# Which engine's queue issues the stores of gV and gK: GpSimd or ScalarE

## The chip, the cores and the metric

The kernel runs on one core of a Trainium2 chip. The core has five engines that run side by side, each with its own queue of instructions: TensorE (PE; its weight loads are PEld), VectorE (DVE), ScalarE (ACT), GpSimd (POOL) and SyncE (SP). An instruction that waits holds up everything behind it in its engine's queue. A transfer between the chip's large memory and the on-chip tiles is issued by an instruction of SP, ACT or POOL and then carried out by 16 DMA engines that all issuers share. The metric is the device time of one execution in microseconds (us).

## The reference

The reference computes one decode step of a transformer block and all its gradients. A query (batch 2, one position, width 640) goes through a layer norm and a projection into 32 heads of 128, attends to caches of 4096 keys and values per head, is projected back and added to x, and goes through a layer norm and a small relu network. What is computed around the change are the gradients of the caches. For one pair (b, h):

```python
scores = einsum("bhqd,bhkd->bhqk", q, k) * (Dh ** -0.5)
p = softmax(scores)
o = einsum("bhqk,bhkd->bhqd", p, v)
```

With one query position, the gradient of v is the outer product of p (4096) and the gradient of o (128), and the gradient of k is the outer product of the scores' gradient (4096) and q (128). Each is a matrix of 4096 x 128 bf16, 1 MiB. There are 64 pairs, so 128 such matrices are written: 134 MB of the 149 MB that the kernel writes. It reads 211 MB, most of it the caches, V being read a second time for 52 of the pairs.

## The kernel before

A tile of 1 MiB is [128 partitions, 32 chunks, 128], 8 KB in each partition.

**Pass 1** (p1_iter, L461) walks over the 64 pairs with three of them in work at a time: pair i has its K transposed on PE and copied out of PSUM by ACT (t_sb, L440) and its scores computed; pair i-1 has its softmax (ep on ACT, L523) and K times ep on VectorE (pk, L476); pair i-2 has its matrix with V on PE (m_ps, L469). It yields between eight segments, k = 0 to 7.

**Pass 2** (p2_iter, L858, and p2_tail, L837) makes the gradients, in the order of the list turns. p2_iter(j) transposes V of its pair (tile W) in four groups on PE, each copied out by ACT (T0 to T3, L440), and multiplies each with the gradient of o (dp). Meanwhile VectorE writes gV in two halves (L832, by outer_half). The dp of the pair is complete only after T3; p2_tail(j) then makes gsp on VectorE (L843) and gK in two halves (L832). p2_tail(j) is run from inside p2_iter(j+1). In the first steps without pass 1, ACT writes the last eight of the 32 chunks of gV (nsb, L899), in the last three steps four.

POOL issues the store of gV at L900 and that of gK at L851, straight behind the last instruction that writes the tile in the program's order, and copies the small tiles pp and pf for the next step (L874, L877). The buffers of gV and gK come from a pool of tiles with the tag "g": take hands one out and give returns it to the list in program order; on the chip, the next writer of the buffer waits until its store has landed. There are three of them while both passes run, and five to ten later.

The order of the work is written out by hand. The plan (L1110) is a list of steps (i, j): pass 1 alone until i = 40, then both, with a new j at every second i; in the last two steps of pass 1 (i = 64 and 65) j = 12 and 13; then pass 2 alone (i is None) from j = 14 on. While both run, p2_step (L1163) is called after chosen segments of p1_iter (HEAVY, LIGHT). In the background, generators do the weights' gradients: outer_rows (L939) has PE make blocks of 512 columns, ACT copy them into ot (L965), and ACT issue their stores (L968, 19 of them). go_group, ga_gen and gx_gen keep VectorE busy with products and sums (L658).

SP issues all loads (L456 for K, V and W). When a buffer comes free, the next load is issued.

Of the kernel before, what the change touches and what calls it, by code (L numbers as in the profile page):

```python
# [15 lines left out]
def kernel(  # L16
# [73 lines left out]
    def take(tag, shape, name):  # L90
        assert free[tag] > 0, (tag, name)
        free[tag] -= 1
        k = homes[tag].pop(0)
        t = pools[k].tile(shape, BF16, tag=f"big{k}", bufs=1, name=name)
        home_of[id(t)] = (tag, k, t)
        return t
# [354 lines left out]
    def natural(cache, b, h):  # L451
        return cache[b, h].rearrange("(p sc) d -> p sc d", sc=NSC)
# [8 lines left out]
    def p1_iter(i, dve_group, busy):  # L461
# [56 lines left out]
            m_part(0)  # L518
            m_part(1)
        yield  # L520
        if p is not None:
            ep = pkp.tile([128, NSC, 2], BF16, tag="ep", bufs=3, name="ep")
            nc.scalar.activation(out=ep[:], in_=p["s"][:, :, None].to_broadcast([128, NSC, 2]),  # L523
                                 func=ACT.Exp, bias=nb[:], scale=SCALE, accum_out=es[:, bp, hp:hp + 1])
            p["ep"] = ep
            p["pk"] = []
            pk_tile(0)
        if c is not None:
            c["KT2"] = pair_transpose(c["K"], 2, busy=busy)
# [304 lines left out]
            in0=row.rearrange("p (a two) -> p a two", two=2)[:, None, :, :].to_broadcast([128, n, 64, 2]),  # L834
            in1=colp[:, sl, None, :].to_broadcast([128, n, 64, 2]), op=ALU.mult)

    def p2_tail(j):  # L837

        p = S2[j]
        bp, hp = turns[j]  # L840
        pair_matvec(p["dp"], p.pop("T3"), 3, gom[:, bp, hp, :, :])
        gsp = small.tile([128, NSC, 2], BF16, tag="gsp", bufs=2, name="gsp")
        nc.vector.scalar_tensor_tensor(  # L843
            out=gsp[:], in0=p["dp"][:, :, None].to_broadcast([128, NSC, 2]), scalar=negdot[:, hp, bp:bp + 1],
            in1=P_bf[:, p_slot[(bp, hp)], :, None].to_broadcast([128, NSC, 2]), op0=ALU.add, op1=ALU.mult)
        yield
        gK = take("g", [128, NSC, 128], "gK")
        outer_half(gK, p["rb"][:, 128:256], gsp, 0)
        yield
        outer_half(gK, p["rb"][:, 128:256], gsp, 1)  # L850
        nc.gpsimd.dma_start(out=natural(out_2, bp, hp), in_=gK[:])  # L851
        give(gK)
        del S2[j]
        yield

    NSB = 8

    def p2_iter(j, nsb):  # L858

        tail = p2_tail(j - 1) if j - 1 in S2 and "T3" in S2[j - 1] else iter(())  # L860
        c = S2[j]
        next(tail, None)
        b, h = turns[j]
        go = gom[:, b, h, :, :]
        bank = pst([128, 512], FP32, "sps", "dp_ps")
        for k, col in enumerate((goc, qsc)):
            nc.tensor.matmul(bank[:, 128 + k * 128:256 + k * 128],  # L867
                             lhsT=col[:, h, b:b + 1].to_broadcast([128, 128]), rhs=ident_bf[:],
                             start=True, stop=True)
        c["dp"] = bank[:, 0:NSC]  # L870
        rb = mats.tile([128, 256], BF16, tag="rb", bufs=3, name="rb")
        nc.scalar.activation(out=rb[:], in_=bank[:, 128:384], func=ACT.Copy, scale=rt[:, b, h:h + 1])  # L872
        pp = small.tile([128, NSC, 2], BF16, tag="pp", bufs=2, name="pp")
        nc.gpsimd.tensor_copy(out=pp[:], in_=P_bf[:, p_slot[(b, h)], :, None].to_broadcast([128, NSC, 2]))  # L874
        if nsb:
            pf = small.tile([128, NSB], FP32, tag="pf", bufs=2, name="pf")
            nc.gpsimd.tensor_copy(out=pf[:, 0:nsb], in_=P_bf[:, p_slot[(b, h)], NSC - nsb:NSC])  # L877
        c.update(rb=rb, pp=pp)
        c["T0"] = pair_transpose(c["W"], 0)
        next(tail, None)  # L880
        yield
        for _ in tail:
            yield
        c["T1"] = pair_transpose(c["W"], 1)
        pair_matvec(c["dp"], c.pop("T0"), 0, go)
        yield
        c["T2"] = pair_transpose(c["W"], 2)
        pair_matvec(c["dp"], c.pop("T1"), 1, go)
        yield
        c["T3"] = pair_transpose(c["W"], 3)  # L890
        give(c["W"], "g" if j < H and j != 1 and owned["g"] < 3 else None)
        pair_matvec(c["dp"], c.pop("T2"), 2, go)
        gV = take("g", [128, NSC, 128], "gV")
        outer_half(gV, c["rb"][:, 0:128], c["pp"], 0)
        yield
        outer_half(gV, c["rb"][:, 0:128], c["pp"], 1, HALF - nsb)
        if nsb:
            for k in range(nsb):
                nc.scalar.activation(out=gV[:, NSC - nsb + k, :], in_=rb[:, 0:128], func=ACT.Copy, scale=pf[:, k:k + 1])  # L899
        nc.gpsimd.dma_start(out=natural(out_3, b, h), in_=gV[:])  # L900
        give(gV)
        yield


# [265 lines left out]
    for n, (i, j) in enumerate(plan):  # L1170
        all_go = all(("go", B - 1, h) in done for h in range(H))
        if i is None and plan[n - 1][0] is not None:
            pkp.release()
            big1 = tc.alloc_tile_pool(name="big1", bufs=1)
            for _ in range(2):
                more_home("ld", big1)
            share(ld=KEPT[1] + 4, g=5)
        if all_go and not late[0]:
            wop.release()
            big3 = tc.alloc_tile_pool(name="big3", bufs=1, side="right")  # L1180
            for tag in ("ld", "g", "g", "q", "q", "q"):
                more_home(tag, big3)
        late[0] = all_go
        more = int(late[0])
        if fin is not None and not bg2 and not bg3:
            share(ld=8 + 3 * more, g=7 + 3 * more)
        elif fin is not None and j >= H:
            held = sum(bh in kept for bh in turns[j + 1:])
            share(ld=5 + held + more, g=5 + 2 * more, f=3, q=2 + 3 * more)
        while g2 is not None:  # L1190
            p2_step()
        open_tail = [k for k in S2 if "T3" in S2[k]]
        if j is not None:
            if j < NP1:
                bg_until(("go", *turns[j]))
            nsb = 0 if i is not None else NSB if j < H and fin is None else NSB // 2 if j >= NP1 - 3 else 0
            g2 = p2_iter(j, nsb) if j < NP1 else p2_tail(NP1 - 1)
        elif open_tail:
            g2 = p2_tail(open_tail[0])
        if i is None and ("w1", 1) in done and fin is None:  # L1200
            wts.release()
            fin = tc.alloc_tile_pool(name="fin", bufs=1)
            big2 = tc.alloc_tile_pool(name="big2", bufs=1)
            more_home("f", big2)
            banks.update(sps=[2, 3], o=[4, 5, 6])
            bg2.append(("fin", fin_gen(fin)))
            bg3.append(("gx", gx_gen(fin)))
        if i == 12:
            bg.append(("ga", ga_gen()))
        if i == H + 2:  # L1210
            banks["bc"].insert(0, banks["sps"].pop(0))
        elif i == P2_AT:
            banks["bc"].remove(7)
            banks["sps"].insert(0, banks["bc"][0])
            banks["bc"] = [7]
        rate = RATES[0 if i is not None and i <= H + 1 else 1 if j is None and i < P2_AT else
                     2 if i is not None else 3 if j <= H else 4]
        if i is None:
            spread[0] = 2
            at_k[0] = 1  # L1220
            k = 0
            while g2 is not None:
                p2_step()
                pump()
                slot[0] = int(k in ((1, 3, 5) if j <= H else (1, 4)))
                k += 1
                bg_step(0, rate)
                bg_step(1, RATE2[int(j >= RATE2_AT)] * (0.4 if spreading[0] else 1.0))
                bg_step(2, RATE3)
            continue  # L1230
        at = LIGHT if j is None else HEAVY_TAIL if open_tail else HEAVY
        for k, _ in enumerate(p1_iter(i, i < H + 1, 0)):
            for _ in range(at.get(k, 0)):
                if g2 is not None:
                    p2_step()
            if k == 5:
                a_heads(i)
            pump()

            spread[0] = 1 if i < P2_AT else 2  # L1240
            at_k[0] = k
            if i >= P2_AT:
                slot[0] = int(k == 6 or (k == 1 and j is None))
            elif i > H + 1:
                slot[0] = {1: 2, 3: 1, 4: 1, 6: 1}.get(k, 0)
            else:
                slot[0] = int(k in (1, 6))
            bg_step(0, rate)
            bg_step(1, 0.0)
        if i is not None and i in (H + 1, NP1 + 1):  # L1250
            bg.append((f"m{i // H - 1}", middle_gen(i // H - 1)))
# [41 lines left out]
```

## Time and profile before

| what | value |
|---|---|
| median of 3 runs | 894.84 us (894.83 to 897.51) |
| the profiled execution | 896.3 us |
| its span on the core | 894.4 us |
| busy: PE, DVE, ACT, POOL | 740.6, 688.1, 469.5, 198.6 us |
| bytes read, written | 211.1 MB, 149.1 MB |
| mean rate over the span | 405 GB/s |
| POOL's DMA queue | 134.2 MB |
| SP's DMA queue | 211.1 MB |
| ACT's DMA queue | 14.9 MB |

The profile is one execution recorded by the hardware. Its page gives each engine's busy time, then the span in 40 equal slices: each digit is the busy share of a slice in tenths, and the lines DMA and GB/s give the mean busy share of the 16 DMA engines and what they moved. Then come the DMA queues, the chain of work that ended last, the costliest groups of instructions (a line L440 is line 440 of the kernel, and t_sb<-t_ps says what is written from what), and the DMA issues with the median time from issue to landing. The same trace can be asked for a line, for a stretch of time, or for all instructions of a stretch in order; there, "[0.56 <-PE t_ps L435]" means that the engine sat idle for 0.56 us until an instruction of PE at L435 was done.

### The profile page before, as it was taken

To read this page: it belongs to the slowest core of one execution; us is meant where nothing else is said; L and a number is where in the kernel's file an instruction comes from. 1 tells how busy PE (TensorE), PEld (TensorE's weight loads), DVE (VectorE), ACT (ScalarE), POOL (GpSimd) and SP (SyncE) were. 2 spreads that over 40 slices of the span, in tenths; PEclk is the share of its full clock that TensorE was granted. 3 is DMA by queue.
4 is the path that set the end of the run, shared out by engine and by line. 5 is a ranking of instruction groups with operands and counts; after the bars stand their busy time and mean duration, and the time that the engine had idled before them with its cause. 6 is when DMAs were issued, how large, how long until landed. Compare 5 with 4: busy or idle time off the path is not lost.

```text
span 894.4 us, 24636 instructions
## 1 busy us (share of the span) xinstructions
PE 740.6 (83%) x10145; PEld 622.7 (70%) x10145; DVE 688.1 (77%) x1283; ACT 469.5 (52%) x1184; POOL 198.6 (22%) x342
## 2 busy tenths in 40 slices
PE   4999899999998998897867887875698988858881
PEld 4887788888887887777757776764566765635570
DVE  2666778976888897796678897877988468898992
ACT  1344334443555665464545776553476666537751
POOL 1344434442210000000011231111222111111141
PEclk9999989999999999898995555555657566555655
DMA  9999999999979999999999999999999999999996
GB/s 377 420 412 403 409 407 418 411 414 410 356 299 366 422 422 424 422 422 423 414 382 390 416 416 418 414 412 422 398 394 423 426 421 424 423 426 424 423 423 256
DMA packets 56304, 361.84 MB, mean 405 GB/s; under 512 B 5696, under 2 KB 11904, under 8 KB 15488
## 3 DMA queue, kind: packets, MB, share of 16 engines
q1 hardware_dynamic: 34536, 211.13, 58.1%
q0 software_dynamic: 18432, 134.23, 36.1%
q10 hardware_dynamic: 3224, 14.92, 4.0%
q8 instruction: 80, 1.31, 0.6%
q14 instruction: 32, 0.26, 0.1%
HBM read 211.11 MB, written 149.13 MB: 403 GB/s over the span
## 4 chain that ended last, share of the span: by engine, by line
DMA 37%; PE 31%; DVE 19%; issue 6%; ACT 3%; POOL 1%; SPq 0%; POOLq 0%; DVEq 0%; ACTq 0%
DMA out_dram<-gK 16%; PE t_ps L435 13%; DMA Vt<-in_A_v_cache_dram 12%; PE m_ps L469 7%; DMA out_dram<-gV 5%; DVE gV L832 5%; DVE gK L832 4%; DVE rows L658 4%; PE s_ps L448 3%; DVE pk L476 3%; DMA wo_t<-in_A_wo_dram 2%; PE u_ps L498 2%; DMA Kt<-in_A_k_cache_dram 2%; PE dp_ps L448 2%; ACT t_sb L440 1%
## 5 line engine op out<-in xcount | busy, mean ns | idle before, releaser
L440 ACT COPY t_sb<-t_ps 128x512 f32<-128x512 f32 x479 | 272.6, 587 | 181.3 <-PE t_ps L435 177.0
L448 PEld LDWEIGHTS <-t_sb 128*128 128x128 bf16 x4096 | 169.7, 103 | 75.1 <-ACT t_sb L440 33.3
L435 PE MATMUL t_ps<-ident_f,Wt 128*128 128x128 f32 x832 | 200.0, 392 | 0.4 <-ACT t_sb L440 0.4
L476 DVE TENSOR_TENSOR pk<-Kt,ep 128x2048 bf16<-128x2048 bf16 x128 | 156.3, 1222 | 44.7 <-ACT ep L523 26.0
L469 PE MATMUL m_ps<-pk,Vt 128*128 128x129 bf16 x2048 | 175.8, 224 | 15.0 <-DMA Vt<-in_A_v_cache_dram 14.4
L832 DVE TENSOR_TENSOR gK<-rb,gsp 128x2048 bf16<-128x2048 bf16 x128 | 153.4, 1224 | 18.5 <-DMA out_dram<-gV 16.9
L832 DVE TENSOR_TENSOR gV<-rb,pp 128x2048 bf16<-128x2048 bf16 (+2 forms) x128 | 147.1, 1172 | 23.6 <-DMA out_dram<-gK 23.1
L435 PEld LDWEIGHTS t_ps<-ident_f,Wt 128*128 128x128 f32 x832 | 140.2, 204 | 32.1 <-issue 26.5
L435 PE MATMUL t_ps<-ident_f,Kt 128*128 128x128 f32 x1024 | 153.4, 285 | 3.7 <-DMA Kt<-in_A_k_cache_dram 3.5
L469 PEld LDWEIGHTS <-Vt 128*128 128x128 bf16 x2048 | 130.9, 100 | 18.1 <-DMA Vt<-in_A_v_cache_dram 16.1
L435 PEld LDWEIGHTS t_ps<-ident_f,Kt 128*128 128x128 f32 x1024 | 116.3, 148 | 5.1 <-issue 2.6
L486 POOL COPY pk<-ep 128x16 bf16<-128x16 bf16 x80 | 83.6, 1047 | 152.3 <-ACT ep L523 107.0
L448 PE MATMUL dp_ps<-gom,t_sb 128*128 128x2 bf16 x2048 | 96.0, 168 | 14.5 <-ACT t_sb L440 14.1
L900 POOL DMA_DIRECT2D out_dram<-gV x64 | 34.3, 536 | 317.7 <-DVE gV L832 115.6
L448 PE MATMUL s_ps<-gom,t_sb 128*128 128x2 bf16 x2048 | 80.2, 164 | 1.2 <-DVE t_sb L438 1.2
L851 POOL DMA_DIRECT2D out_dram<-gK x64 | 34.1, 533 | 200.3 <-DVE gK L832 149.6
L582 ACT CAST MT<-m_ps 128x128 bf16<-128x128 f32 x64 | 17.0, 266 | 116.3 <-PE m_ps L469 116.3
L965 ACT CAST ot<-o_ps 128x512 bf16<-128x512 f32 (+3 forms) x152 | 66.8, 494 | 8.9 <-DMA out_dram<-ot 7.3
L872 ACT ACTIVATE rb<-dp_ps,rt 128x256 bf16<-128x256 f32 x64 | 30.3, 474 | 45.5 <-PE dp_ps L867 43.2
L658 DVE CUSTOM_DVE_ANT_0 rows<-wo_t,rows 128x640 bf16<-128x640 bf16 x64 | 52.3, 818 | 0.2
L658 DVE CUSTOM_DVE_ANT_0 rows<-wqs,gqr 128x1024 bf16<-128x1024 bf16 x40 | 48.8, 1220 | 0.2
L658 DVE CUSTOM_DVE_ANT_0 rows<-w_t,rows 128x640 bf16<-128x640 bf16 (+2 forms) x58 | 45.9, 792 | 2.8 <-ACT rows L636 2.1
(194 smaller groups left out, 715.7 us busy)
## 6 DMA issues: line engine op xcount, KB each, us to landing
Kt<-in_A_k_cache_dram SPq DMA_DIRECT2D x64, 1024.0 KB, 16.5
Vt<-in_A_v_cache_dram SPq DMA_DIRECT2D x64, 1024.0 KB, 16.6
out_dram<-gV POOLq DMA_DIRECT2D x64, 1024.0 KB, 14.1
out_dram<-gK POOLq DMA_DIRECT2D x64, 1024.0 KB, 14.3
Wt<-in_A_v_cache_dram SPq DMA_DIRECT2D x52, 1024.0 KB, 11.4
out_dram<-ot ACTq DMA_DIRECT2D x6, 960.0 KB, 12.7
wq_t<-in_A_wq_dram SPq DMA_DIRECT2D x5, 1024.0 KB, 11.0
wqs<-in_A_wq_dram SPq DMA_DIRECT2D x5, 1024.0 KB, 22.2
```

The source lines that it names most:

```text
L435: nc.tensor.transpose(t_ps[:, j, :], natf[:, 2 * cc:2 * cc + 2, :].rearrange("p c k -> p (c k)"), ident_f[:])
L440: nc.scalar.copy(out=t_sb[:], in_=t_ps[:])
L448: nc.tensor.matmul(dst[:, sc:sc + 2], lhsT=v[:, j, :, par], rhs=vecs[:, par, :], start=(par == 0), stop=(par == 1))
L469: nc.tensor.matmul(r["m"][:, 0:129], lhsT=r["V"][:, sc, :], rhs=r["pk"][sc // HALF][:, sc % HALF, 0:129], start=(sc == 0), stop=(sc == NSC ...
L476: nc.vector.tensor_tensor(out=p["pk"][k][:, :, 0:128].rearrange("p s (a two) -> p s a two", two=2), in0=p["K"][:, sl, :].rearrange("p s (a ...
L486: nc.gpsimd.tensor_copy(out=col, in_=e)
L658: nc.vector.tensor_tensor_reduce(out=junk[0:kc, 0:width], in0=in0, in1=in1, scale=1.0, scalar=0.0, op0=ALU.mult, op1=ALU.add, accum_out=acc)
L832: nc.vector.tensor_tensor(out=pairs_view(dst[:, sl, :]), in0=row.rearrange("p (a two) -> p a two", two=2)[:, None, :, :].to_broadcast([128 ...
L851: nc.gpsimd.dma_start(out=natural(out_2, bp, hp), in_=gK[:])
L872: nc.scalar.activation(out=rb[:], in_=bank[:, 128:384], func=ACT.Copy, scale=rt[:, b, h:h + 1])
L900: nc.gpsimd.dma_start(out=natural(out_3, b, h), in_=gV[:])
L965: nc.scalar.copy(out=ot[0:P, k, n0:n0 + nn], in_=o_ps[0:P, 0:nn])
```

## The change

No store of gV or gK is issued where its tile is finished any more. The tile and its destination are put on a list, unsent, and a function send issues everything on that list from ACT's queue and gives the tiles back. send is called in four places:

- in p1_iter, in the third segment (k = 2), behind ep's activation, or in the same place where there is no pair i-1;
- in p2_iter when pass 1 is over (lone): once behind the copy of T0, which finds the gV of the step before, and once behind the copy of T2, which finds the gK of the step before;
- in the last p2_tail, behind gsp for the last gV;
- in the last p2_tail, behind the second half of gK for the last gK.

What is computed, and the number and shape of the stores, stay the same; POOL keeps its copies.

```diff
+            send()
             pk_tile(0)
...
+    unsent = []
+
+    def send():
+
+        while unsent:
+            dst, t = unsent.pop(0)
+            nc.scalar.dma_start(out=dst, in_=t[:])
+            give(t)
+
-    def p2_tail(j):
+    def p2_tail(j, alone=False):
...
         yield
+        if alone and j == NP1 - 1:
+            send()
         gK = take("g", [128, NSC, 128], "gK")
...
         outer_half(gK, p["rb"][:, 128:256], gsp, 1)
-        nc.gpsimd.dma_start(out=natural(out_2, bp, hp), in_=gK[:])
-        give(gK)
+        unsent.append((natural(out_2, bp, hp), gK))
         del S2[j]
+        if alone and j == NP1 - 1:
+            send()
         yield
...
-    def p2_iter(j, nsb):
+    def p2_iter(j, nsb, lone):
...
         c["T0"] = pair_transpose(c["W"], 0)
+        if lone:
+            send()
         next(tail, None)
...
         c["T2"] = pair_transpose(c["W"], 2)
+        if lone:
+            send()
         pair_matvec(c["dp"], c.pop("T1"), 1, go)
...
-        nc.gpsimd.dma_start(out=natural(out_3, b, h), in_=gV[:])
-        give(gV)
+        unsent.append((natural(out_3, b, h), gV))
         yield
...
-            g2 = p2_iter(j, nsb) if j < NP1 else p2_tail(NP1 - 1)
+            g2 = p2_iter(j, nsb, i is None) if j < NP1 else p2_tail(NP1 - 1, True)
```

More of the change, by code (lines that the diff above doesn't have):

```diff
@@ L520, in p1_iter @@
         yield
-        if p is not None:
+        if p is None:
+            send()
+        else:
             ep = pkp.tile([128, NSC, 2], BF16, tag="ep", bufs=3, name="ep")
@@ L887, in p2_iter @@
         c["T2"] = pair_transpose(c["W"], 2)
+        if lone:
+            send()
         pair_matvec(c["dp"], c.pop("T1"), 1, go)
```

## Prediction

> **What bounds the kernel now.** I read the page from the top: busy shares, slices, then the trace by stretches, by issues, and in order of time. PE is busy 83% and DVE 77% of the span, but the slices say that neither is the limit.
>
> ```profile
> DMA  9999999999979999999999999999999999999996
> GB/s 377 420 412 403 409 407 418 411 414 410 356 299 366 422 422 424 422 422 423 414 382 390 416 416 418 414 412 422 398 394 423 426 421 424 423 426 424 423 423 256
> ```
>
> The 16 DMA engines are at work almost everywhere, at about 424 GB/s where loads and stores run together. The view by stretches shows where they are not (stretch, length, busy us of PE, PEld, DVE, ACT, POOL, granted clock, DMA share, GB/s).
>
> ```profile
> 224.00:291.00 67.00, 61.93 (x1043) 54.55 (x1041) 56.53 (x140) 36.76 (x101) 10.40 (x20) 0.97 0.88 340
> 291.00:445.00 154.00, 134.72 (x2216) 120.01 (x2214) 120.35 (x248) 85.71 (x231) 12.58 (x29) 0.93 1.01 423
> 445.00:495.00 50.00, 38.12 (x561) 33.64 (x560) 37.88 (x74) 25.74 (x67) 10.16 (x22) 0.73 0.97 386
> 495.00:855.00 360.00, 284.54 (x2646) 218.58 (x2644) 296.28 (x462) 222.94 (x505) 66.80 (x133) 0.57 1.01 418
> 855.00:883.00 28.00, 17.46 (x174) 15.03 (x174) 22.65 (x35) 12.23 (x28) 11.77 (x17) 0.50 1.01 423
> 883.00:894.40 11.40, 0.00 (x0) 0.00 (x0) 0.00 (x0) 0.00 (x0) 0.00 (x0) 0.50 0.23 98
> ```
>
> All 128 stores are issued after 265 us. Of that time the DMA engines are full (share 1.01) in 291 to 445 and 495 to 883: there a store that is issued later only waits less in its queue. Only in 265 to 291, in 445 to 495 and in the drain after 883 can the moment of an issue reach the end.
>
> **What moves.** 128 issues of 1 MiB leave POOL (533 ns each at L851 and L900) for ACT, which already issues the stores of ot:
>
> ```profile
> L968 ACTq DMA_DIRECT2D out_dram<-ot x19: 338/351/546, 571.4 to 850.6; - x19
> ```
>
> So 128 x 0.351 = 45 us more on ACT, busy 469.5 of 894.4 us; POOL loses 68 us that bound nothing; SP's loads stay. In the trace the packets of a POOL store begin 3.7 us after its issue when its queue is empty, those of an ot store from ACT 3.6: the path itself brings nothing. The landing times look otherwise (issues between 570 and 860 us; last column, median us to landing):
>
> ```profile
> out_dram<-gV POOLq DMA_DIRECT2D x33, 1024.0 KB, 20.8
> out_dram<-gK POOLq DMA_DIRECT2D x33, 1024.0 KB, 21.1
> ...
> out_dram<-ot ACTq DMA_DIRECT2D x6, 960.0 KB, 12.7
> ```
>
> That is no faster queue: in the packets of the engine that ends last the queues take turns, and POOL's holds three to five stores where ACT's holds one. Stores that share ACT's queue share its turn.
>
> **When the new issue comes.** POOL issues a store 0.3 us after the tile's last write. The new points are behind ep in steps of pass 1, later behind the first and third t_sb copy of the next p2_iter. For each store I compared the end of that ACT instruction with POOL's issue. While pass 1 runs, gV is 0.25 us later and gK mostly 1 us, at most 6. Afterwards about 60 of 102 are later, by 0.2 to 4.6 us. The other 40 are negative, by up to 10 us: ACT is there before VectorE is done and must wait, with its next t_sb copies, rb and ot casts queued behind it, and PE behind those.
>
> **The terms**, where the DMA engines have room:
>
> 1. 265 to 291 us. The first gK store goes at 275.12; ep ends at 276.57, 1.45 us later. Loads run beside it (share 0.97 in 275 to 280): 0 to 1.45 us, taken as 0.4.
>
> 2. 445 to 495 us, the hand-over to pass 2 alone, on three buffers for gV and gK. VectorE waits for each landing:
>
> ```profile
> 460.20 2.36 DVE L832 TENSOR_TENSOR gK<-rb,gsp 128x2048 bf16<-128x2048 bf16 x2 [1.45 <-DMA out_dram<-gV]
> ...
> 465.12 2.36 DVE L832 TENSOR_TENSOR gV<-rb,pp 128x2048 bf16<-128x2048 bf16 x2 [2.56 <-DMA out_dram<-gK]
> ...
> 469.99 1.23 DVE L832 TENSOR_TENSOR gK<-rb,gsp 128x2048 bf16<-128x2048 bf16 x1 [2.31 <-DMA out_dram<-gV]
> ...
> 471.54 0.67 PE L605 MATMUL a_ps<-OFc,wo_t 128*128 128x1 bf16 x20 [8.10 <-DVE OFc L596]
> ...
> 474.10 0.59 ACT L440 COPY t_sb<-t_ps 128x512 f32<-128x512 f32 x1 [9.98 <-PE t_ps L435]
> ```
>
> The reader sees one chain: three landings 4.9 us apart, OFc queued behind VectorE's waits, PE idle 8 us for OFc, ACT idle 10 us for PE. The store behind 465.12 is the gK that POOL issued at 454.16. In the new order it is sent in the next step of pass 1, k = 2, behind the t_sb copy that ends at 458.6: 4.5 us later, just ahead of the gV that went at 458.85. The earlier gV (451.29) goes 1.3 us later and lands at about 461.4. The stores' queue is then empty until about 462.5 (458.9 + 3.6), and the next landings come at about 468.7 and 473.6 (4.9 us each, plus 1.3 for the slowest engine) instead of 465.1 and 470.0. PE resumes 3.6 us later. Do the loads fill this? SP issues a Wt at 461.8 and the next at 476.3, when PE has freed a tile, so no. Bounds 0 (hidden) and 4.7 (the whole delay); I take 3.5.
>
> 3. 475 to 495 us: ACT sets the pace, as it also writes eight blocks of each gV; the step repeats after 6.39 us.
>
> ```profile
> 505.26 2.46 ACT L899 ACTIVATE gV<-rb,pf 128x128 bf16<-128x128 bf16 x8
> ...
> 507.97 0.58 ACT L440 COPY t_sb<-t_ps 128x512 f32<-128x512 f32 x1
> ...
> 511.17 0.59 ACT L440 COPY t_sb<-t_ps 128x512 f32<-128x512 f32 x1 [0.56 <-PE t_ps L435]
> ```
>
> One issue falls behind the first copy (507.97) and pushes the second; the other fits into the 0.56 us ahead of the fourth. So 0.35 us for some four steps: 0 to 1.4, 2.8 if both count; I take 0.5. From 495 us on this costs nothing: a step moves 3.146 MB, 492 GB/s at 6.39 us and 467 at 6.74, above what the engines give either way.
>
> 4. Full stretches: 0. Their cover is the queue of stores; if it empties, rival A is the price.
>
> 5. The end: the last gK is issued right behind VectorE, as before (878.33). 0, between -0.4 (POOL's closing drain has no store of its own) and +0.6 (the last gV).
>
> Sum 0.4 + 3.5 + 0.5 = +4.4 us, bounds -0.4 and +9.6 (1.45 + 4.7 + 2.8 + 0.6). The profiled execution took 896.3 us (span 894.4 and 1.9 around it), 1.5 above the median, 894.84. So 900.7 for an execution like it, and **899.2** beside the median.
>
> **Rivals.**
>
> A, slower: ACT is held by VectorE in the full stretches. Place: where ACT is ahead, about 585 to 640 us (by up to 10 us), 763 to 790 (5) and 836 to 875 (5).
>
> ```profile
> 620.29 0.47 ACT L872 ACTIVATE rb<-dp_ps,rt 128x256 bf16<-128x256 f32 x1 [6.01 <-PE dp_ps L867]
> ```
>
> VectorE waits there for landings (23.1 us ahead of gV, 16.9 ahead of gK in all), and ACT would wait with it, losing a lead of some 20 us. If half is missed later, +10 on the forecast: 909. Against it: behind a send ACT needs 0.35 + 0.59 us and PE 0.6 for the next gsp, while VectorE has 2.4 us of gV to do. It decides where the DMA share in 495 to 855 falls below 0.99.
>
> B, not slower: the late DMA engine catches up.
>
> ```profile
> 885.00:888.00 3.00, 0.00 (x0) 0.00 (x0) 0.00 (x0) 0.00 (x0) 0.00 (x0) 0.50 0.25 104
> 888.00:891.00 3.00, 0.00 (x0) 0.00 (x0) 0.00 (x0) 0.00 (x0) 0.00 (x0) 0.50 0.07 30
> ```
>
> 0.25 is four engines of 16, 0.07 is one: it works until 892.3. With 0.23 of 11.4 us left at 883, equal engines would end at 885.6. If POOL's queue makes it late and ACT's does not, 4 to 6.7 us come off: 892.5 to 895.2, or 888 to 891 if term 2 is hidden too. For it: a POOL store's last share lands up to 12 us behind its first, an ot store's 2. Against it: from 855 us on, with almost nothing but POOL's stores, its packets follow at 0.306 us like the others', and it falls no further behind.
> The Trainium skill (DMA: Bandwidth & Descriptors, "Latency and other measured facts") calls two of the engines usually slower and, as a best guess, blames the software-built descriptor rings, hence only GpSimd's issues. By that rule B would come about; the steady rate after 855 us does not bear it out.
>
> C, slower: ACT's issue is held with many stores outstanding. SP's issues at L456 take 0.33 us but up to 10.96 behind seven loads, one of them in rows of 1,280 bytes. Some twenty issues between 735 and 800 us held 1 us each, half of it felt: +10, 909. Against it: behind seven plain loads of 1 MiB SP also took 0.33.
>
> D: the hand-over hides its delay and the terms vanish: 895 to 896.
>
> **Numbers.** Forecast 0.47, A 0.18, B 0.18, C 0.07, D 0.10. About 0.3% (2.7 us) is what a measurement can tell from no change. Of the forecast, 0.10 lies within it (term 2 under 1.8 us); B is half faster, half within; D within; A and C slower. Faster 0.09, same 0.10 + 0.09 + 0.10 = 0.29, slower 0.37 + 0.25 = 0.62. The range takes in the sum's bounds (894.4 to 904.4), B's upper half and A's and C's price: 891 to 909.
>
> **What would show it.** Right: VectorE's waits for landings around 465 us grow and PE resumes near 475; DMA share 1.01 in 495 to 855; ACT's issues at 0.35 us. Towards A: long waits of ACT for gV and gK. Towards B: all engines ending within 3 us. Towards C: ACT issues over 1 us. What I trust least is term 4.

## The result and the profile after

| | before | after |
|---|---|---|
| median (lowest to highest), 8 runs each | 897.14 us (894.83 to 898.88) | 900.34 us (899.01 to 903.38) |
| profiled execution, its span | 896.3 us, 894.4 us | 900.27 us, 898.4 us |
| busy: PE, DVE, ACT, POOL | 740.6, 688.1, 469.5, 198.6 us | 737.6, 686.9, 468.9, 129.9 us |

The changed kernel takes 1.0045 of the time before (95% interval 1.0027 to 1.0063). By that ratio and by the means of the eight runs it is about 4 us slower, by the medians 3.2. The busy times of the computing engines hardly differ; POOL's falls by 69 us, about its 128 issues (68 us).

The slices of the changed kernel (mean busy share of the 16 DMA engines in tenths, and GB/s, 22.5 us each):

```profile
DMA  9999999999979999999998999999999999999997
GB/s 379 419 411 405 408 408 418 410 414 406 352 284 361 423 423 423 421 422 423 410 349 356 413 425 423 414 416 408 408 401 410 412 425 426 424 425 423 421 412 299
```

The same by stages (first two columns the stretch and its length in us, then the busy time of PE, PEld, DVE, ACT, POOL, then TensorE's granted clock, the DMA share and GB/s):

```profile
291.00:445.00 154.00, 133.54 (x2195) 118.53 (x2196) 119.52 (x244) 83.26 (x226) 2.13 (x9) 0.94 1.01 422
445.00:500.00 55.00, 39.98 (x589) 35.43 (x590) 39.13 (x79) 27.25 (x72) 3.40 (x11) 0.69 0.92 356
500.00:855.00 355.00, 276.27 (x2567) 211.28 (x2566) 288.14 (x450) 215.36 (x491) 26.76 (x47) 0.56 1.01 418
...
889.00:892.00 3.00, 0.00 (x0) 0.00 (x0) 0.00 (x0) 0.00 (x0) 0.00 (x0) 0.50 0.80 336
892.00:895.00 3.00, 0.00 (x0) 0.00 (x0) 0.00 (x0) 0.00 (x0) 0.00 (x0) 0.50 0.13 55
895.00:898.40 3.40, 0.00 (x0) 0.00 (x0) 0.00 (x0) 0.00 (x0) 0.00 (x0) 0.50 0.03 14
```

The full stretches are as full as before, 1.01 at 422 and 418 GB/s. What sinks is the hand-over, 0.92 at 356 GB/s, where the kernel before has 0.98 at 389 in 445 to 500 us. At the end 0.13 is two engines of 16 and 0.03 is less than one.

To place the loss I added up the bytes of all DMA packets in the order in which they end, and asked how much later each sum is reached than in the profiled kernel before. The columns name the time of that sum in the kernel before:

| us behind, at | 281 | 447 | 499 | 619 | 740 | 881 | last landing | span |
|---|---|---|---|---|---|---|---|---|
| after | +1.2 | +1.4 | +5.8 | +5.1 | +5.5 | +6.3 | +4.6 | +4.0 |

So 1.4 us before the hand-over, 4.4 in it, about 0.5 in the 380 us behind it, then 1.7 back from 881 us to the last landing, while the queues empty, and 0.6 back after it.

The hand-over of the changed kernel, in order of time (start, duration, engine, line; in brackets the idle time ahead and what ended it; L835 is L832 of before, L846 is send):

```profile
460.16 0.34 ACTq L846 DMA_DIRECT2D out_dram<-gK  x1
...
462.38 2.36 DVE L835 TENSOR_TENSOR gK<-rb,gsp 128x2048 bf16<-128x2048 bf16 x2 [1.63 <-DMA out_dram<-gV]
...
471.35 2.36 DVE L835 TENSOR_TENSOR gV<-rb,pp 128x2048 bf16<-128x2048 bf16 x2 [6.61 <-DMA out_dram<-gK]
...
475.39 1.22 DVE L835 TENSOR_TENSOR gK<-rb,gsp 128x2048 bf16<-128x2048 bf16 x1 [1.48 <-DMA out_dram<-gV]
...
476.95 0.67 PE L608 MATMUL a_ps<-OFc,wo_t 128*128 128x1 bf16 x20 [11.45 <-DVE OFc L599]
...
479.51 0.58 ACT L440 COPY t_sb<-t_ps 128x512 f32<-128x512 f32 x1 [13.33 <-DVE h L756]
```

gK of step 11, whose last half ends at 455.9, is sent at 460.16. The gV that needs its buffer waits 6.61 us for the landing instead of 2.56, and the chain behind it is the one of before: OFc, PE (idle for 11.45 us instead of 8.10), ACT.

### The profile page after: what moved, and what is told of

The parts are those of the page before. It is cut to its first block, busy times and chain, and to the rows that moved or that the text cites. A ratio compares the mean times of both kernels' runs of the same rounds, so it can differ in the third digit from the quotient of the medians.

```text
span 898.4 us, 24577 instructions
## 1 busy us (share of the span) xinstructions
PE 737.6 (82%) x10145; PEld 617.5 (69%) x10145; DVE 686.9 (76%) x1283; ACT 468.9 (52%) x1184; POOL 129.9 (14%) x214
## 4 chain that ended last, share of the span: by engine, by line
PE 36%; DMA 30%; DVE 20%; ACT 6%; issue 4%; ACTq 1%; SPq 1%; DVEq 0%
PE t_ps L435 16%; DMA Vt<-in_A_v_cache_dram 10%; PE m_ps L469 7%; DMA out_dram<-gK 6%; DMA out_dram<-ot 5%; DVE gK L835 5%; DVE gV L835 5%; DVE rows L661 4%; DMA Kt<-in_A_k_cache_dram 4%; DVE pk L476 3%; PE s_ps L448 3%; PE o_ps L977 3%; DMA wo_t<-in_A_wo_dram 2%; PE u_ps L498 2%; ACT t_sb L440 2%
## 5 line engine op out<-in xcount | busy, mean ns | idle before, releaser
L435 PE MATMUL t_ps<-ident_f,Wt 128*128 128x128 f32 x832 | 198.0, 389 | 0.2 <-ACT t_sb L440 0.2
L835 DVE TENSOR_TENSOR gK<-rb,gsp 128x2048 bf16<-128x2048 bf16 x128 | 152.9, 1220 | 11.1 <-DMA out_dram<-gV 9.4
L835 DVE TENSOR_TENSOR gV<-rb,pp 128x2048 bf16<-128x2048 bf16 (+2 forms) x128 | 147.0, 1171 | 9.8 <-DMA out_dram<-gK 9.6
L889 POOL COPY pp<-P_bf 128x64 bf16<-128x64 bf16 x64 | 28.9, 452 | 564.1 <-DVE gV L835 553.2
L855 DVE SCALAR_TENSOR_TENSOR gsp<-dp_ps,negdot,P_bf 128x64 bf16<-128x64 f32 x64 | 17.9, 279 | 42.3 <-PE dp_ps L448 42.2
## 6 DMA issues: line engine op xcount, KB each, us to landing
wqs<-in_A_wq_dram SPq DMA_DIRECT2D x5, 1024.0 KB, 13.6
```

The costliest lines, as they stand in the source:

```text
L435: nc.tensor.transpose(t_ps[:, j, :], natf[:, 2 * cc:2 * cc + 2, :].rearrange("p c k -> p (c k)"), ident_f[:])
L835: nc.vector.tensor_tensor(out=pairs_view(dst[:, sl, :]), in0=row.rearrange("p (a two) -> p a two", two=2)[:, None, :, :].to_broadcast([128 ...
```

## The experiments

**Theory**: the whole loss is the hand-over, where a late store keeps VectorE from its third buffer. **Rivals**: the loss is spread over ScalarE's 128 issues (rival A); or it belongs to the queue, whoever waits. Each ratio is to the kernel before, run on the same chip.

| run | median us | before | ratio | 95% interval |
|---|---|---|---|---|
| e1, gK of step 11 sent in place | 897.13 | 896.32 | 1.0006 | 0.9991 to 1.0021 |
| e2, before with two late stores | 900.62 | 896.32 | 1.0053 | 1.0033 to 1.0074 |
| e3, ScalarE in pass 1 only | 903.60 | 896.32 | 1.0085 | 1.0066 to 1.0104 |
| e4, ScalarE after pass 1 only | 896.80 | 896.32 | 1.0003 | 0.9991 to 1.0016 |
| e5, before with a fourth buffer | 897.84 | 896.85 | 1.0011 | 0.9996 to 1.0025 |
| e6, after with a fourth buffer | 897.45 | 896.85 | 1.0011 | 0.9998 to 1.0023 |
| e7, ScalarE issues at once | 926.48 | 896.85 | 1.0334 | 1.0306 to 1.0363 |
| e8, e3 with gK of step 11 in place | 900.12 | 896.85 | 1.0033 | 1.0015 to 1.0052 |
| e9, e8 with ScalarE's last two | 899.54 | 896.70 | 1.0034 | 1.0022 to 1.0047 |
| e10, at once in pass 2 alone | 911.13 | 896.70 | 1.0173 | 1.0151 to 1.0194 |
| e11, at once up to step 32 | 897.52 | 896.85 | 1.0012 | 0.9996 to 1.0028 |

And the time by which their bytes are behind the kernel before, from one profiled run each:

| us behind, at | 281 | 447 | 499 | 619 | 740 | 881 | last landing | span |
|---|---|---|---|---|---|---|---|---|
| e1 | +1.4 | +1.7 | +2.1 | +1.8 | +2.2 | +3.8 | +2.4 | +1.7 |
| e2 | +2.1 | +2.1 | +8.8 | +7.9 | +7.4 | +7.8 | +7.6 | +7.5 |
| e3 | +0.8 | +1.2 | +2.2 | +1.4 | +2.0 | +2.1 | +2.3 | +5.6 |
| e4 | +0.6 | +0.6 | -0.1 | +1.3 | +3.1 | +4.1 | +1.7 | +1.3 |
| e5 | +1.4 | +2.8 | +0.1 | -1.2 | -1.2 | -0.7 | -0.2 | -0.2 |
| e6 | +1.1 | +5.1 | +3.1 | +3.1 | +2.2 | +4.0 | +2.4 | +1.8 |
| e7 | +2.0 | +17.5 | +19.8 | +20.0 | +30.9 | +40.7 | +34.5 | +33.8 |
| e8 | +1.7 | +1.8 | +1.6 | +0.8 | +1.2 | +1.5 | +1.5 | +4.7 |
| e9 | +2.0 | +2.3 | +2.2 | +1.6 | +1.6 | +1.7 | +1.7 | +4.9 |
| e10 | -0.8 | -0.6 | -2.1 | -2.0 | +7.8 | +17.5 | +11.6 | +10.9 |
| e11 | +1.9 | +2.2 | +1.2 | +0.7 | +5.1 | +6.2 | +3.4 | +2.7 |

Two warnings. Each row is one execution, and not always a typical one: those of e2, e7 and e9 were the slowest of their runs, those of e3 and e10 the fastest. And in the first column e2, e4 and e5 run the instructions of the kernel before up to the hand-over, and still stand 0.6 to 2.1 us behind it at 281 us: a profile differs from the next by that much there.

**e1, one store undone.**

```diff
-        if alone and j == NP1 - 1:
+        if j == 11 or alone and j == NP1 - 1:
             send()
```

> The changed kernel, but the one gK store of step 11, which the change sends about 4 us later at the hand-over from pass 1 to pass 2, is issued from ScalarE straight behind VectorE's last half. Theory 'hand-over': nearly all of the loss is that one store, so some 3 us of the 4 come back: ratio to the kernel before about 1.001 (897.5 to 898.5 where before is 897.1), and PE resumes near 475 us instead of 478. Rival 'held ScalarE' (ScalarE waiting for VectorE in the full stretches): no gain, ratio stays at 1.0045.

The loss is gone: 1.0006. Its hand-over:

```profile
456.28 0.34 ACTq L846 DMA_DIRECT2D out_dram<-gK  x1
...
461.57 2.36 DVE L835 TENSOR_TENSOR gK<-rb,gsp 128x2048 bf16<-128x2048 bf16 x2 [0.43 <-DMA out_dram<-gV]
...
466.07 2.36 DVE L835 TENSOR_TENSOR gV<-rb,pp 128x2048 bf16<-128x2048 bf16 x2 [2.14 <-DMA out_dram<-gK]
...
471.38 1.23 DVE L835 TENSOR_TENSOR gK<-rb,gsp 128x2048 bf16<-128x2048 bf16 x1 [2.76 <-DMA out_dram<-gV]
...
472.94 0.67 PE L608 MATMUL a_ps<-OFc,wo_t 128*128 128x1 bf16 x20 [6.63 <-DVE OFc L599]
```

The store goes 3.9 us earlier than in the changed kernel, the long wait is 2.14 us again, and PE gets OFc 4.0 us earlier. The other 127 stores still go from ScalarE where the change sends them, most of them late, and their cost in time is within the interval (0.9991 to 1.0021).

**e2, the reverse.** The kernel before; only gK of step 11 and gV of step 12 go through send.

```diff
-        nc.gpsimd.dma_start(out=natural(out_2, bp, hp), in_=gK[:])
-        give(gK)
+        if j == 11:
+            unsent.append((natural(out_2, bp, hp), gK))
+        else:
+            nc.gpsimd.dma_start(out=natural(out_2, bp, hp), in_=gK[:])
+            give(gK)
```

> The kernel before, with only two of the 128 stores moved: gK of step 11 and gV of step 12 are issued from ScalarE at the place where the change sends them, in the last step of pass 1; all others stay on GpSimd. Theory 'hand-over': these two alone cost about 3 us, ratio 1.0035, and the bytes moved fall 3 us behind between 445 and 500 us. Rival 'held ScalarE': ratio 1.000, since ScalarE issues two stores only. Third possibility, the delay is hidden by loads: 1.000 as well, but with VectorE's waits for landings grown.

1.0053: two stores of 128 bring the whole loss. The long wait is there again, and longer:

```profile
473.15 2.36 DVE L834 TENSOR_TENSOR gV<-rb,pp 128x2048 bf16<-128x2048 bf16 x2 [8.65 <-DMA out_dram<-gK]
```

In this trace, of the slowest of the six runs, 6.7 us arise between 447 and 499 us. By its ratio e2 loses a little more than the change itself, but the intervals don't separate the two; here the two queues also share the DMA engines, and the gV issued at 460.50 took 18.3 us to land, against 13.6 in the changed kernel.

**e3 and e4, the change split at the end of pass 1.** In e3 ScalarE issues only while pass 1 runs and GpSimd afterwards; in e4 the other way round. The edit of e3 at gV (that at gK is alike, and e4 has "not lone"):

```diff
-        unsent.append((natural(out_3, b, h), gV))
+        if lone:
+            nc.gpsimd.dma_start(out=natural(out_3, b, h), in_=gV[:])
+            give(gV)
+        else:
+            unsent.append((natural(out_3, b, h), gV))
```

> The change up to the end of pass 1 (stores of steps 0 to 12, and gV of 13, from ScalarE where the change sends them), and GpSimd's immediate issue afterwards. Theory 'hand-over': at least four fifths of the loss stay, ratio 1.0035 to 1.005. Rival 'held ScalarE': most of the loss goes, ratio about 1.001.

> The complement: GpSimd's immediate issue until pass 1 is over, and ScalarE's delayed issue for the 100 or so stores after it. Theory 'hand-over': hardly any loss, ratio 0.999 to 1.0015, though the moments at which ScalarE and VectorE work shift by several us after 585 us. Rival 'held ScalarE': nearly the whole loss, ratio 1.0035.

e4 speaks against rival A as the cause of this loss: with 101 stores from ScalarE the time is that of the kernel before, 1.0003. That nothing was lost on the way can't be said. In e4's trace VectorE holds ScalarE for 24.8 us, and between 499 and 881 us its bytes fall 4.2 us behind, of which 2.4 come back by the last landing. The other kernels divide in the same way: between 499 and 881 us those with ScalarE's stores there lose 0.5 (the changed kernel), 0.9 (e6), 1.7 (e1) and 5.0 us (e11, below; e7 and e10 far more), while those with GpSimd's gain 0.1 to 1.0 (e2, e3, e5, e8, e9). It is one execution of each.

But e3 is slower than the whole change. Its trace shows why: the last landing is only 2.3 us behind the kernel before, the end of the program 5.6. GpSimd's closing drain (the DRAIN instruction next to its last issue, in the kernel before from 878.3 to 893.7 us) lasts until 4.6 us after the last landing, against 1.4 in the kernel before. That is a second cost, which belongs to e3 and not to the change. The hand-over is smaller in this trace than the theory has it: the gK goes 3.4 us later than in the kernel before, VectorE's two waits grow to 3.02 and 5.08 us and PE gets OFc 2.8 us later, yet the bytes fall only 1.0 us behind between 447 and 499 us. With 4.4 us in the changed kernel and 6.7 in e2, a single trace fixes the price of the late store poorly; the timings below do it better.

**e8 and e9, e3's surplus.** e8 is e3 with the store of e1 in place; in e9 ScalarE issues the last two stores as well (second and third part of the diff).

```diff
-        if alone and j == NP1 - 1:
+        if j == 11 or alone and j == NP1 - 1:
             send()
...
-        if lone:
+        if lone and j < NP1 - 1:
             nc.gpsimd.dma_start(out=natural(out_3, b, h), in_=gV[:])
...
-p2_tail(NP1 - 1, True, True)
+p2_tail(NP1 - 1, True)
```

> ScalarE issues the stores only while pass 1 runs, as in the run before that had a ratio of 1.0085, but gK of step 11 is sent where it is finished. Theory, the hand-over accounts for 0.4% of that and the rest is the end: there GpSimd's last instruction, a drain, ended 4.6 us after the last store had landed, against 1.4 us in the kernel before. So with the hand-over mended the ratio is 1.002 to 1.005, and the drain again ends 4 us or more after the last landing. Rival, the late end was chance in that one profile and all loss was in the hand-over: 0.999 to 1.002, drain 1 to 2 us behind the last landing.

> As the run before with ScalarE's issues in pass 1 only and gK of step 11 sent in place (ratio 1.0033), but ScalarE's queue also issues the last two stores of the kernel, so that GpSimd's last store lands some 5 us earlier. Theory, the 0.33% is GpSimd's last drain, which there ended 4.6 us after GpSimd's last landing (1.3 us in kernels where it issues 126 to 128 stores): now that end lies beside the last two transfers, and the ratio is 0.999 to 1.002. Rival, the two queues beside each other cost transfer time: about 1.003 again.

e8: 1.0033. Against e3 the one store in place takes off 0.5% (1.0085 to 1.0033), and the late end is there again: span 4.7 us behind, last landing 1.5. e9 was to uncover the drain, and failed in that: GpSimd's last store, though issued ahead of the other two, still landed with the last packets of all, at 894.03, and the drain ended 4.5 us later. The end of GpSimd's drain behind its last landing in all six kernels where it issues to the end: 1.4, 1.3 and 1.4 us (before, e2, e5: 126 to 128 stores) and 4.6, 4.6 and 4.5 us (e3, e8, e9: 99 to 101). That it is the drain is read from the traces; what makes it longer stays open.

**e5 and e6, a fourth buffer** for gV and gK from step 62 of the plan on (NP1 - 2 in the edit, NP1 being 64; the first expectation below says step 64), taken from the loads; e5 is the kernel before, e6 the changed one.

```diff
-            give(p["K"], "g" if i == P2_AT else None)
+            give(p["K"], "g" if i in (P2_AT, NP1 - 2) else None)
```

> The kernel before, GpSimd still issuing every store, with a fourth buffer for gV and gK from step 64 of the plan on (the K buffer freed there goes to them instead of to the loads). Theory, the hand-over's landing waits on three buffers cost transfer time in the kernel before too: its share of the DMA engines was 0.97 from 445 to 495 us against 1.01 on both sides, so at most 50 x 0.04 / 1.01 = 2.0 us are to be had; ratio to before 0.998 to 1.000, and VectorE's waits for landings at 462 to 470 us gone. Rival, the loads feel the buffer that they lose: 1.002 or more.

> The changed kernel with the same fourth buffer. Theory, the change loses its time because the late store of gK of step 11 keeps VectorE from its third buffer: with a fourth one the delay has no reader, the share of the DMA engines from 445 to 500 us goes from 0.92 to 0.96 or more, and the ratio to before is 0.998 to 1.001. Rival, the loss is the two stores' own time in the queue (each engine is empty while they are late, whoever waits): about 1.003 to 1.0045 as without the buffer.

With the buffer the change is no slower than the kernel before with it, 1.0011 each: the late store costs where the next writer of its buffer waits for it. In e6 VectorE writes the gK and the gV for which it waited 1.63 and 6.61 us in the changed kernel without a wait, and waits at the next gK:

```profile
460.42 2.36 DVE L835 TENSOR_TENSOR gK<-rb,gsp 128x2048 bf16<-128x2048 bf16 x2
462.70 2.35 DVE L835 TENSOR_TENSOR gV<-rb,pp 128x2048 bf16<-128x2048 bf16 x2
...
471.18 1.23 DVE L835 TENSOR_TENSOR gK<-rb,gsp 128x2048 bf16<-128x2048 bf16 x1 [5.93 <-DMA out_dram<-gK]
```

The traces show the price too. Both kernels gain 2.0 to 2.7 us between 447 and 499 us, where the change alone loses 4.4. But at 447 us they have lost 1.4 (e5) and 4.0 us (e6) against their own first columns, where the loads have one tile less: the Wt that SP issues at 437.0 us in the kernel before and at 438.2 in the changed one goes at 447.2 in e5 and at 449.6 in e6, and from 440 to 450 us e6 moves 285 GB/s where the changed kernel moves 384. So what e5 was to gain is taken back ahead of it. In e6's trace the share from 445 to 500 us is 0.94, not the 0.96 that I had expected, and the longest wait for a landing 5.9 us: the buffer helps without clearing the hand-over.

**e7, no delay.** The kernel before, with ScalarE as the issuer at both places and nothing else.

```diff
-        nc.gpsimd.dma_start(out=natural(out_2, bp, hp), in_=gK[:])
+        nc.scalar.dma_start(out=natural(out_2, bp, hp), in_=gK[:])
...
-        nc.gpsimd.dma_start(out=natural(out_3, b, h), in_=gV[:])
+        nc.scalar.dma_start(out=natural(out_3, b, h), in_=gV[:])
```

> The kernel before with ScalarE's queue in place of GpSimd's at both stores and nothing delayed: ScalarE issues each store straight behind the last write of its tile in the program's order, so it stands waiting for VectorE's last half each time, 128 times. Theory, the hand-over is the whole loss and ScalarE's waits elsewhere are covered by the DMA engines' own queue: 0.999 to 1.003, the DMA share from 500 to 855 us still 1.00 or more. Rival, ScalarE held behind VectorE holds up the loads (rival A of the prediction): 1.005 to 1.02, and that share under 0.99.

My theory fell here, and by far: 1.0334, 30 us. In the trace of e7, ScalarE while both passes run:

```profile
306.98 0.34 ACTq L900 DMA_DIRECT2D out_dram<-gV  x1
307.41 1.08 ACT L440 COPY t_sb<-t_ps 128x512 f32<-128x512 f32 x2 [1.95 <-DVE gsp L843]
...
313.94 0.34 ACTq L851 DMA_DIRECT2D out_dram<-gK  x1
314.32 0.27 ACT L582 CAST MT<-m_ps 128x128 bf16<-128x128 f32 x1 [3.42 <-DVE gK L832]
```

ScalarE stands 3.42 us until VectorE has written gK, and the copies of both passes stand behind it. In the changed kernel the same issue comes behind ep and starts with it, with no gap:

```profile
307.77 0.31 ACT L525 ACTIVATE ep<-s_ps,nb 128x64 bf16<-128x64 f32 x1
307.77 0.34 ACTq L846 DMA_DIRECT2D out_dram<-gK  x1
```

So rival A's mechanism is real, and the DMA engines' queue does not cover it; the few segments of delay avoid most of it. ScalarE's idle time that ends with VectorE's gV, gK or gsp is 0.5 us in the kernel before, 11.9 in the changed one, 24.8 in e4, 51.2 in e10 (below) and 103.7 in e7. The sign that I had named, a share under 0.99 from 500 to 855 us, is a poor one: e7 has 0.99 there, at 403 GB/s where the kernel before has 417.

**e10 and e11, where it bites.** Both have e1's store in place, and the delay in pass 1. e10 issues at once in all of pass 2 alone, e11 only up to step 32 (there the conditions also ask for j <= H, and the last gK stays as it was). The diff of e10 against e1:

```diff
-        if j == 11 or alone and j == NP1 - 1:
+        if j == 11 or j > 12:
             send()
...
         unsent.append((natural(out_3, b, h), gV))
+        if lone:
+            send()
```

> The changed kernel with gK of step 11 sent where it is finished (ratio 1.0006 by itself), and, once pass 1 is over, every store issued by ScalarE straight behind the last write of its tile, not a few segments later; in pass 1 the delay stays. Theory, in the run with no delay at all (1.0334) the cumulative bytes fell behind by 17.5 us before 447 us and by 20 us after 640 us, each part from ScalarE standing behind VectorE in that stretch: ratio 1.015 to 1.025. Rival, only pass 1 is hurt and what came later was its consequence: 1.000 to 1.006.

> The changed kernel with gK of step 11 sent where it is finished and, from the end of pass 1 to step 32 of pass 2 alone (about 620 us), every store issued at once; before and after that the delay stays. In the run with all of pass 2 alone at once (1.0173) the cumulative bytes were 2.1 us ahead of the kernel before at 499 us and stayed so to 619 us; they fell behind by 9.7 us from 640 to 716 us and by 9.3 us from 834 to 881 us. Theory, the loss is ScalarE held by VectorE where the weights' gradients share both engines: without those stretches the ratio is 0.997 to 1.001. Rival, any store issued at once costs: 1.003 or more.

e10: 1.0173, about half of e7's loss, and by its bytes all of it after 619 us. From 640 to 740 us, the kernel before and then e10:

```profile
640.00:740.00 100.00, 86.20 (x838) 66.55 (x839) 74.56 (x114) 68.01 (x148) 21.35 (x39) 0.61 1.01 417
```

```profile
640.00:740.00 100.00, 78.18 (x738) 57.73 (x737) 66.79 (x106) 60.20 (x129) 2.61 (x11) 0.60 0.95 374
```

PE, VectorE and ScalarE each do 9 to 12% less in the same 100 us, and the DMA engines move 10% less. e11, without those stretches, is back at 1.0012: an issue at once up to step 32 costs nothing that can be measured, and its bytes lose nothing up to 619 us. Its centre lies just above the 1.001 that I had named. Its trace falls 4.4 us behind between 619 and 740 us, though, where the delay is back, and regains 2.8 us from 881 us to the last landing; why it loses more there than the changed kernel (0.4 us) is open. That VectorE's and ScalarE's work on the weights' gradients makes the late stretches tender fits the place; since ot casts run from 560 to 620 us too, without loss, it isn't shown. No version that I tried beats the kernel before.

## Why the prediction was right

The forecast was +4.4 us; the two profiled executions differ by 4.0, and the ratio gives 0.0045 x 897.14 = 4.0. Nearly all of it came out of the step that was named.

- **Term 1, the first gK** (0.4 taken, up to 1.45): not decided. The change is 1.2 us behind at 281 us, but kernels with the old instructions there are behind by 0.6 to 2.1.
- **Term 2, the hand-over** (3.5): right in mechanism and nearly in size. The store was forecast 4.5 us late behind a copy ending at 458.6. It is 6.0 us late by the clock (454.16 to 460.16), some 2 of which the changed kernel's pass 1 was late already at 452 us (ep). The stores' queue ran empty as forecast: gV issued at 453.90 was done at 461.81, gK's first packet began at 463.97. PE resumes with OFc at 476.95 instead of 471.54, 5.4 us later, 3.4 without those 2; e1 puts it at 4.0. Bytes behind: 4.4 us. By timing, e1 says 1.0045 - 1.0006, or 3.5 us (its interval is some 2 us to either side). The traces with the late store spread from 1.0 us (e3) to 6.7 (e2), so the size is less sure than the place.
- **Term 3, ACT's loop** (0.5): too small to see. rb is 5.2 us late at 486 us and 4.9 at 527; nothing is added per step.
- **Term 4, nothing in the full stretches**: right in time (e4 at 1.0003) and nearly so in the changed kernel's bytes (0.5 us in 380), but the cover that I named is thin. The 11.9 us for which VectorE holds ScalarE here hardly show; the 24.8 of e4 go with 4.2 us of bytes, more than half of which the end gives back; 51.2 (e10) already cost 14, and 103.7 (e7) 30. I had read 40 stores from the old trace for which ScalarE would be there first, by up to 10 us; on the chip its idle times were 11, the longest 3.3 us.
- **Term 5, the end** (0, -0.4 to +0.6): the program ends 1.5 us after the last landing instead of 2.1, as GpSimd's closing drain is over long before (875.1): -0.6, just outside the bound. The stretch ahead of it gave back 1.7 us (rival B).
- **Rival A**: hardly in this kernel (0.5 us), but its mechanism is real, and its price of some 10 us was not too high: e10 pays 14 (911.13 - 896.70). Its deciding sign should have been GB/s.
- **Rival B**: some of it came, 1.7 us of its 4 to 6.7. Between 881 us and the last landing, five kernels whose last stretch has ScalarE's stores regain 1.4 to 2.8 us on the kernel before (after, e1, e4, e6, e11; e7 and e10 compute some 20 us longer and don't compare). In those that have GpSimd's there the lag changes by -0.2 to +0.5 us (e2, e3, e5, e8, and e9 but for its last two stores). I had refused B for the steady packets. That the forecast is so close is partly luck: this gain and the 1.4 us that the changed kernel was behind at 447 us nearly cancel. But one engine still ends late, by the windows 892 to 898.4 of after. The Trainium skill (DMA: Bandwidth & Descriptors, "Latency and other measured facts") calls two engines usually slower and guesses that only GpSimd's software-built descriptors are to blame. The shorter drain agrees with part of that; the late engine that is left, with no store from GpSimd, is not explained by it.
- **Rival C**: refuted. ScalarE's issues in the changed kernel (min/median/max ns):

```profile
L846 ACTq DMA_DIRECT2D out_dram<-gV x64: 338/338/901, 269.9 to 883.2; - x64
L846 ACTq DMA_DIRECT2D out_dram<-gK x64: 338/338/1271, 277.2 to 885.7; - x64
```

The median is 0.34 us, and of ScalarE's 149 issues two last over 1 us.

- **Rival D**: refuted; the loads did not fill the gap (0.92, 356 GB/s).

## What to carry to other kernels

When a store is moved to a later point, look for the one place where its buffer's next writer is already waiting and the DMA engines have room; there the delay was paid nearly in full here, elsewhere little of it or nothing. Two of 128 stores were enough for the whole loss, and one line in that place took it away. If a busy engine is to issue transfers of what another engine writes, issue them where the data is surely ready: the same issues without the delay cost seven times as much (1.0334 against 1.0045).

## What the runs showed of the hardware

- GpSimd's closing drain ended 1.3 to 1.4 us behind its last landing with 126 to 128 stores, and 4.5 to 4.6 us with 99 to 101 stores of which ScalarE had issued the others. The two kernels with that late end and gK of step 11 in place are 0.3% slower (1.0033 and 1.0034). It was seen only in the three kernels in which ScalarE issued the first 27 stores (in e9 the last two as well), not with two stores from ScalarE (e2); the cause is open.
- A DMA share near 1 does not mean the full rate: from 500 to 855 us e7 moved 403 GB/s at 0.99 where the kernel before moved 417 at 1.01.
